# Loading weight chunks in pairs, converting their bits in 1024 columns, and giving block 0 six first steps of FFN1

## The chip, the cores and the metric
The kernel runs on one core of a Trainium2 chip. The metric is the device time in microseconds (us); lower is better. Every time here comes from the chip's runs or from the trace of one profiled execution.

## The reference
A masked attention over 4 batches, 8 heads, 576 tokens of 64 dimensions feeds two feed-forward networks, each over 2304 tokens of width 512:

```
scores = q @ k.T / 8 ; heads 0..3: keys 0..31 back ; heads 4..7: every fourth key, 0..127 back
attn   = exp(scores - max) / (sum + 1e-9)
x      = (attn @ v) as [2304, 512]
h = x @ w_in                                   # FFN1, 512 -> 2048
g = where(h > 0, h, exp(min(h, 0)) - 1)
x = g @ w_out                                  # 2048 -> 512
out = ((x @ w_a) * (x @ w_b)) @ w_out2         # FFN2, 512 -> 1536 -> 512
```

q, k and v are float32; the weights reach the kernel as float64.

## The kernel before, in words
**Tiles and stages.** The tokens are cut into 6 blocks of 384. Attention works per block and head pair p (4 pairs, two heads each), FFN1 per block and column chunk f of 128 (16 chunks). One step (block, f) of FFN1 is 12 matmuls of 384 columns into one PSUM tile (`h1_mm`, L656), the ELU on ScalarE and VectorE (relu L678, exp L679, maximum L684, then a split of g into a high and a low part, L667 and L669), and two steps later 12 matmuls into the block's four output tiles (`y1_mm`, L703). Three products (high·high, high·low, low·high) make up each matmul of the reference, which is why a step has 24. FFN2 (L1123, L1458) follows on all blocks with fewer products by a Strassen-like scheme.

**Order of FFN1.** `STEPS1` lists the steps: block 0 does its first SPLIT steps, then block 1 all 16, then block 0 the rest, then blocks 2 to 5. The weights of chunk f, ("1i", f) of w_in and ("1o", f) of w_out, are loaded and converted for the first SPLIT chunks during block 0's steps, for the others during block 1's.

**Converting weights.** A raw chunk of 128x512 float64 numbers (512 KB) comes as two words each into a tile `wraw`, four of which exist. `bits` makes float32 of it in five instructions of 512 columns: magnitude of the high word (ScalarE, L281), low word scaled (ScalarE, L286), clamp (VectorE, L291), join of both words (VectorE, L296), sign (VectorE, L299). Then the high part (ScalarE, L307) and the low part (VectorE, L321 or L1003) go into a tile `w`. Up to SPLIT the chunks are converted at steps written in the code (`w_convert`), later ones by a planner that fills each step's room on ScalarE and VectorE (`Op`, `COST`, `ROOM`, `tick`), keeping the planned load ahead of use. FFN2's weights go through the same planner and then into combinations that the scheme needs.

**Attention.** Blocks 0 and 1 are the "early" ones, 2 to 5 "steady". For each pair there are scores (early L429, steady L603), softmax, transposes (L515, L623), a copy pt of them (ScalarE, L521), values (L539, L639), and a split of the result into x's high part (ScalarE, L556) and low part (VectorE, L557). In early scores and values, as in steady scores, a matmul reads one half of the 128 partitions, and the program's text alternates between halves. In early values the two halves write two tiles (`banks`). At which FFN1 step each piece is put in is set by the tables B1, B2, B3 and by `end` for the transposes of block 1, which come at end + 1, and its values, at end + 2. For pairs 2 and 3 of block 1, b0 is 1 and 2.

**Order on the engines.** Within and between these places a scheduler arranges the instructions of the program, so that neighbouring groups may be cut and interleaved; the final order on an engine is not that of the text. PE runs its queue in that order.

Of the kernel before, what the change touches and what calls it, by code (L numbers as in the profile page):

```python
# [26 lines left out]
TB = 384  # L27
# [9 lines left out]
SPLIT = 7  # L37
# [9 lines left out]
NRAW = 4  # L47
# [7 lines left out]

C1, C0, AHEAD, LAG_IN, LAG_OUT = SPLIT, NF1 + SPLIT, 56, 3, 1
# [185 lines left out]
def banded_attention_two_ffn(ctx: ExitStack, tc: tile.TileContext, ins, out):  # L242
# [20 lines left out]

    def w_load(key, behind=None):
        kind, f = key
        raw = pm.tile([128, 512, 2], U32, tag="wraw", name="wraw", bufs=NRAW)
        if behind is not None:
            with tc.issue_after(behind):
                G.memset(raw[:, :1, 0], 0)
        SP.dma_start(  # L270
            out=raw.rearrange("p f h -> p (f h)"), in_=ins["w" + kind][f].bitcast(U32)
        )
        w_raw[key] = raw
# [37 lines left out]
    def w_convert_parts(key, pool, on):  # L311

        raw = w_raw.pop(key)
        t = pm.tile([128, 512], U32, tag="wt", name="wt", bufs=4)
        w = pools[pool].tile([128, 2, 512], F32R, tag="w", name="w")
        w_sb[key] = w
        steps = bits(raw[:, :, 1], raw[:, :, 0], t, on[0])
        t = t.bitcast(F32)
# [4 lines left out]
        return [*steps, lambda: part_hi(on[1], w[:, 0, :], t), lower]  # L323

    def w_convert(keys, pool, on):

        for steps in zip(*[w_convert_parts(key, pool, on) for key in keys]):
            for step in steps:
                step()
# [22 lines left out]
    early = Env("at0", ps0, n_early, "right")  # L352
    m_at = [0, 128 + TB, 128 + 2 * TB, ins["masks_e"].shape[1]]
# [418 lines left out]
    free = ["w"] * 11  # L772
# [19 lines left out]
    y2_t = {}  # L792

    def y2_temp(S, op):
        if S and op == "t4":
            y2_t[op] = [pm.tile([128, 512], F32, tag="wt", name="yt", bufs=4) for _ in range(2)]
        elif S:
            y2_t[op] = pm.tile([128, 2, TB], F32, tag="wraw", name="yt", bufs=NRAW)
# [101 lines left out]
    n_free, tail = {"wraw": NRAW, "wt": 4}, [False]  # L900
# [91 lines left out]
    def chunk_ops(key):  # L992

        at = {}
        x = assembly(at)(key)

        def hi():
            at["to"] = pools["wb"].tile([128, 2, 512], F32R, tag="w", name="w")
            part_hi("A", at["to"][:, 0, :], at["t", key])

        def lo():
            w = w_sb[key] = at["to"]
            V.tensor_tensor(w[:, 1, :], at["t", key], f32(w[:, 0, :]), op=SUB)  # L1003

        give("wraw", x)
        give("wt", Op("V", 512, lo, Op("A", 512, hi, x)))

    def assembly(at):
        def assemble(key):
# [3 lines left out]
            def load():  # L1013
                raw = pm.tile([128, 512, 2], U32, tag="wraw", name="wraw", bufs=NRAW)
                SP.dma_start(
                    out=raw.rearrange("p f h -> p (f h)"),
                    in_=ins["w" + key[0]][key[1]].bitcast(U32),
                )
                at["raw", key] = raw

            def high():
                raw = at["raw", key]
                t = pm.tile([128, 512], U32, tag="wt", name="wt", bufs=4)
                chunk.extend(bits(raw[:, :, 1], raw[:, :, 0], t, "A"))
                at["t", key] = t.bitcast(F32)
                at["w", key] = raw.rearrange("p f h -> p (f h)").bitcast(F32)
# [11 lines left out]
    def unit_ops(j):  # L1038
# [17 lines left out]
        def combine(M):  # L1056
# [14 lines left out]
            def spare2():  # L1071
                if "hi" not in at:
                    at["hi"] = pm.tile([128, 512], U32, tag="wt", name="wt", bufs=4).bitcast(F32)
                return at["hi"]

            def spare3():
                if "hi3" not in at:
                    at["hi3"] = pm.tile([128, 512], U32, tag="wt", name="wt", bufs=4).bitcast(F32)
                return at["hi3"]

            on = ON3[M]
            at.pop("hi", None)
            x0, x1 = assemble(k0), assemble(k1)
            if M == "o":
                s1 = add(0, lambda: t(0, 1), lambda: t(0, 0), SUB, x0, x1)
# [4 lines left out]
            else:  # L1090
                s1 = add(0, lambda: t(1, 0), lambda: t(1, 1), ADD, x0, x1)
# [190 lines left out]
    o_ps, o_acc = {}, {}  # L1282
# [64 lines left out]
    def o_parts(S, j, first, last):  # L1347
# [35 lines left out]
        def temp(name):  # L1383
            t = o_acc[name] = pm.tile([128, 512], F32, tag="wt", name="ot", bufs=4)
            return t
# [454 lines left out]
```

## Time and profile before

| | us |
|---|---|
| median of 3 runs | 888.05 (887.69 to 888.75) |
| profiled execution | 887.98 |
| its span | 886.1 |
| PE busy | 879.5 (99%) |
| VectorE busy | 645.2 (73%) |
| ScalarE busy | 499.6 (56%) |

The 1.9 us by which the execution exceeds its span lie around the work that the trace records. PE is TensorE's matmuls, DVE is VectorE, ACT is ScalarE, POOL is GpSimd. A timeline's row is a run of instructions of one kind: its start, its duration to the end of the last one, and in brackets idle time and who ended it. The last matmul's end overlaps the next row's start, so that the price of a group on PE is best read from start to start. The attention's float32 matmuls of scores and values appear as two passes each in the trace, so that a group of 12 has a count of 24; in the order they are counted once.

### The profile page before, as it was taken

Reading aid. Unit: us, or ns where it says so; the run is one execution under the profiler, and the core shown is the slowest. Engines: PE = TensorE matmul, PEld = TensorE weight load, DVE = VectorE, ACT = ScalarE, POOL = GpSimd, SP = SyncE. Lnnn points to the kernel's source line nnn. Section 1 sums busy time; section 2 is a strip of 40 time slices with the busy share of each in tenths; the row PEclk is TensorE's granted clock in tenths of the full one; section 3 lists DMA queues with packets and bytes.
Section 4 is the critical chain, followed back from the end, with each engine's and each line's share of the span. In section 5 each row is a group of like instructions: output and inputs, shape, how many; then the busy total and the mean of one; then the engine's idle time right before and its main releaser. Section 6 shows DMA issues by size and latency. Waiting matters only on the chain.

```text
span 886.1 us, 17826 instructions
## 1 busy us (share of the span) xinstructions
PE 879.5 (99%) x6669; PEld 850.8 (96%) x6669; DVE 645.2 (73%) x1160; ACT 499.6 (56%) x1214; POOL 223.4 (25%) x219
## 2 busy tenths in 40 slices
PE   8999999999999999999999999999999999999998
PEld 5799999999999999999999999999999999999998
DVE  6998997786777777776885556698656698656666
ACT  6897897866767776677764332236332225332231
POOL 1000012332222332322322222222522222522223
PEclk9999999999999999999999999999999999999999
DMA  8865654766556665548997777767777664777712
GB/s 317 296 204 182 185 182 156 226 217 229 185 185 207 209 196 196 188 132 280 327 352 277 235 252 249 247 217 245 256 279 251 248 204 166 264 267 251 249 68 72
DMA packets 76247, 198.21 MB, mean 224 GB/s; under 512 B 8320, under 2 KB 22656, under 8 KB 76160
## 3 DMA queue, kind: packets, MB, share of 16 engines
q1 hardware_dynamic: 66944, 182.64, 60.9%
q10 hardware_dynamic: 9216, 14.42, 4.8%
q8 instruction: 53, 0.87, 0.4%
q14 instruction: 34, 0.28, 0.1%
HBM read 153.51 MB, written 43.52 MB: 222 GB/s over the span
## 4 chain that ended last, share of the span: by engine, by line
PE 96%; ACT 1%; DVE 1%; DMA 1%; issue 0%; SPq 0%; POOL 0%; DVEq 0%; POOLq 0%; ACTq 0%
PE ps_h L1123 30%; PE ps_h L656 22%; PE ps_y L703 22%; PE ps_o L1458 14%; PE ps_v L639 2%; PE ps_s L603 1%; PE ps_t L623 1%; PE ps_o L1318 1%; PE ps_v L539 1%; DMA qk<-in_qk_d 1%; PE ps_s L429 0%; PE ps_v L502 0%; PE ps_t L515 0%; ACT w L307 0%; ACT e L463 0%
## 5 line engine op out<-in xcount | busy, mean ns | idle before, releaser
L1123 PE MATMUL ps_h<-y,w 128*128 128x384 f32 x1512 | 291.4, 336 | 0.0
L1123 PEld LDWEIGHTS ps_h<-y,w 128*128 128x128 f32 x1512 | 256.5, 188 | 1.4 <-DVE el L1178 0.6
L656 PE MATMUL ps_h<-x,w 128*128 128x384 f32 x1152 | 221.6, 339 | 0.5 <-ACT x L556 0.4
L703 PE MATMUL ps_y<-g,w 128*128 128x384 f32 x1152 | 221.3, 339 | 0.0
L656 PEld LDWEIGHTS ps_h<-x,w 128*128 128x128 f32 x1152 | 199.2, 188 | 3.2 <-ACT x L556 0.7
L703 PEld LDWEIGHTS ps_y<-g,w 128*128 128x128 f32 x1152 | 199.7, 188 | 2.5 <-ACT el L678 0.9
L1458 PE MATMUL ps_o<-w,g 128*128 128x256 f32 x1071 | 152.3, 281 | 0.0
L1458 PEld LDWEIGHTS ps_o<-w,g 128*128 128x128 f32 x1071 | 146.6, 188 | 0.2 <-POOL g L1165 0.2
L669 POOL TENSOR_TENSOR g<-el,g 128x384 fp32r<-128x384 f32 x73 | 80.0, 1096 | 208.1 <-ACT g L667 179.0
L684 DVE SCALAR_TENSOR_TENSOR el<-el,ps_h 128x384 f32<-128x384 f32 x96 | 52.9, 551 | 74.1 <-ACT el L679 73.7
L678 ACT ACTIVATE el<-ps_h 128x384 f32<-128x384 f32 x96 | 46.7, 487 | 49.3 <-PE ps_h L656 49.2
L1481 DVE TENSOR_TENSOR acc<-acc,ps_o 128x512 f32<-128x512 f32 (+1 forms) x77 | 49.6, 644 | 33.9 <-PE ps_o L1458 33.7
L1165 POOL TENSOR_TENSOR g<-el,g 128x384 fp32r<-128x384 f32 x34 | 38.9, 1145 | 124.5 <-ACT g L1164 93.3
L406 POOL TENSOR_TENSOR e<-e,rs 128x288 f32<-128x288 f32 (+1 forms) x32 | 25.9, 809 | 151.1 <-DVE rs L405 151.1
L667 ACT ACTIVATE g<-el 128x384 fp32r<-128x384 f32 x96 | 49.6, 516 | 23.9 <-DVE el L684 23.6
L299 DVE SCALAR_TENSOR_TENSOR wt<-wraw,wt 128x512 uint32<-128x512 uint32 x68 | 57.9, 856 | 0.7
L679 ACT ACTIVATE el<-el 128x384 f32<-128x384 f32 x96 | 50.5, 526 | 2.3
L296 DVE SCALAR_TENSOR_TENSOR wt<-wt,wraw 128x512 uint32<-128x512 uint32 x68 | 46.4, 688 | 3.9 <-ACT wraw L286 0.7
L1174 ACT COPY el<-ps_h 128x384 f32<-128x384 f32 x36 | 17.3, 480 | 54.0 <-PE ps_h L1123 51.8
L397 ACT ACTIVATE e<-e,nm 128x96 f32<-128x96 f32 (+1 forms) x96 | 36.3, 380 | 18.9 <-DVE nm L395 18.8
L281 ACT ACTIVATE wt<-wraw 128x512 f32<-128x512 f32 x68 | 45.3, 666 | 2.4 <-DMA wraw<-in_w1i 2.3
L1213 DVE TENSOR_TENSOR u<-ps_h,u 128x384 f32<-128x384 f32 x36 | 20.0, 557 | 34.1 <-PE ps_h L1123 34.0
(120 smaller groups left out, 1034.0 us busy)
## 6 DMA issues: line engine op xcount, KB each, us to landing
w<-w2P_o SPq DMA_DIRECT2D x52, 512.0 KB, 5.8
w<-w2P_a SPq DMA_DIRECT2D x48, 512.0 KB, 4.3
w<-w2P_b SPq DMA_DIRECT2D x48, 512.0 KB, 4.5
wraw<-in_w1i SPq DMA_DIRECT2D x16, 512.0 KB, 3.6
wraw<-in_w1o SPq DMA_DIRECT2D x16, 512.0 KB, 3.6
wraw<-in_w2a SPq DMA_DIRECT2D x12, 512.0 KB, 4.2
wraw<-in_w2b SPq DMA_DIRECT2D x12, 512.0 KB, 4.3
wraw<-in_w2o SPq DMA_DIRECT2D x12, 512.0 KB, 4.5
```

The source lines that it names most:

```text
L296: V.scalar_tensor_tensor(t, t, 3, L, op0=ALU.logical_shift_left, op1=ALU.bitwise_or)
L299: V.scalar_tensor_tensor(t, H, 0x80000000, t, op0=ALU.bitwise_and, op1=ALU.bitwise_or)
L656: T.matmul(ps[:, :TB], w[:, wi, kc * 128 : (kc + 1) * 128], xs[kc][:, xi, :], start=(n == 0), stop=(n == 3 * KC - 1),)
L667: A.activation(g[:, 0, :], gf, AF.Copy)
L669: last_lo[0] = eng.tensor_tensor(g[:, 1, :], gf, f32(g[:, 0, :]), op=ALU.subtract)
L678: A.activation(e, ps[:, :TB], AF.Relu, scale=-1.0)
L679: last_e[0] = A.activation(e, e, AF.Exp, scale=-1.0)
L684: last_g[0] = V.scalar_tensor_tensor(e, e, -1.0, h_ps.pop(s)[:, :TB], op0=ALU.add, op1=ALU.max)
L703: T.matmul(y_ps[t][c][:, :TB], w[:, wi, c * 128 : (c + 1) * 128], g[:, gi, :], start=(first and n == 0), stop=(last and n == 2),)
L1123: last_mm[0] = T.matmul(ps[:, :TB], w[:, wi, kc * 128 : (kc + 1) * 128], y2[S, yop][kc][:, xi, :], start=(start and n == 0), stop=(n == 5) ...
L1458: T.matmul(ps[:, 256 * n : 256 * n + 256], g[name][:, gi, i * 128 : (i + 1) * 128], w[:, wi, h, :], start=((first or not held) and n == m ...
L1481: V.tensor_tensor(a, a, ps[:, :n], op=ADD)
```

## The change
Raw chunks are loaded two into one tile: two tiles of [128, 2, 512, 2] in place of four of [128, 512, 2], with a second pool of two such tiles while block 0's first steps run. `mates` says which two chunks share a tile. The five bit instructions run once for both chunks, over 1024 columns; the split into high and low parts stays at 512 columns per chunk. The planner takes two chunks at a time, with costs for 1024 columns. SPLIT falls from 7 to 6, and with it the number of early `w` tiles from 16 to 14. The temporaries of FFN2 take halves of the new tiles. Block 1's `end` for its pairs 2 and 3 falls by one step. The core of the diff:

```diff
-SPLIT = 7
+SPLIT = 6
...
-NRAW = 4
+NPAIR = 2
...
+    def mates(key):
+
+        kind, f = key
+        if key in (("1i", SPLIT), ("1i", SPLIT + 1)):
+            return ("1i", SPLIT), ("1i", SPLIT + 1)
+        if kind == "i" or kind == "1i" and f < 2:
+            return ("1i", 0), ("1i", 1)
+        if key in (("1o", SPLIT - 2), ("1o", SPLIT - 1)):
+            return ("1o", SPLIT - 2), ("1o", SPLIT - 1)
+        f -= 2 * (kind == "1i")
+        return ("1o", f), ("1i", f + 2)
...
+        ks = mates(key)
+        if ks not in w_raw:
+            here, there = (pm, {"bufs": NPAIR}), (pools["raws"], {})
+            pool, n = there if ks[0] in EXTRA else here
+            w_raw[ks] = pool.tile([128, 2, 512, 2], U32, tag="wraw", name="wraw", **n)
+        raw = w_raw[ks][:, ks.index(key)]
...
+    def pair_convert_parts(ks, pool, on):
+
+        raw, t = w_tiles(ks)
+        steps = bits(raw[..., 1], raw[..., 0], t, on[0])
+        split = zip(*[split_parts(k, t[:, i].bitcast(F32), pool, on) for i, k in enumerate(ks)])
+        return [*steps, *[fn for fns in split for fn in fns]]
...
+        if keys[0] in ONE or mates(keys[0]) != tuple(keys):
+            parts = zip(*[w_convert_parts(key, pool, on) for key in keys])
+            steps = [step for steps in parts for step in steps]
+        else:
+            steps = pair_convert_parts(tuple(keys), pool, on)
+        for step in steps:
+            step()
...
+    pools["raws"] = ps0.enter_context(tc.tile_pool(name="raws", bufs=NPAIR, side="right"))
...
-    free = ["w"] * 11
+    free = ["w"] * 9 + ["wb"] * 2
...
-    COST = {("A", 512): 0.67, ("V", 512): 0.7, ("G", 512): 1.45}
+    COST = {("A", 1024): 1.1, ("V", 1024): 1.22}
...
-        give("wt", Op("V", 512, lo, Op("A", 512, hi, x)))
+        give("wt", *[split(key) for key in keys])
...
+                raw = pm.tile([128, 2, 512, 2], U32, tag="wraw", name="wraw", bufs=NPAIR)
+                for i, key in enumerate(keys):
+                    SP.dma_start(
+                        out=raw[:, i].rearrange("p f h -> p (f h)"),
+                        in_=ins["w" + key[0]][key[1]].bitcast(U32),
+                    )
+                at["raw", keys] = raw
...
-            b = Op("A", 512, high, a, takes="wt")
-            c = Op("A", 512, lambda: chunk[1](), b)
+            b = Op("A", 1024, high, a, takes="wt")
+            c = Op("A", 1024, lambda: chunk[1](), b)
             d = Op("V", 512, lambda: chunk[2](), b)
-            e = Op("V", 512, lambda: chunk[3](), c, d)
-            return Op("V", 512, lambda: chunk[4](), e)
+            e = Op("V", 1024, lambda: chunk[3](), c, d)
+            return Op("V", 1024, lambda: chunk[4](), e)
 
...
+    later_keys = []
     for f in range(NF1):
         st = f
         ks = [("1o", f)]
         if f + 2 < (SPLIT if f < SPLIT else NF1):
             ks.append(("1i", f + 2))
         if f >= SPLIT:
-            for k in ks[::-1]:
-                chunk_ops(k)
+            later_keys.extend(ks)
+            if len(later_keys) > 1:
+                chunk_ops(tuple(later_keys[::-1]))
+                later_keys.clear()
...
             if t < EARLY:
-                end = b0 + 1 + int(b0 >= 0)
+                end = b0 + 1
```

The scheduler's order on PE, first block 1's values of pairs 2 and 3 (ps_v names the tiles, one for each half of the partitions; pt the transposed weights of attention; ps_y and ps_h FFN1's sums). Before, the transposes and the values of pair 2:

```order
L515 MATMUL ps_t_1038<-ident_82,e_822 128x128 x3
L539 MATMUL ps_v_1044<-pt_993,v_879 64x32 x12
L539 MATMUL ps_v_1045<-pt_993,v_879 64x32 x12
L703 MATMUL ps_y_859<-g_954,w_958 128x384 x2
L703 MATMUL ps_y_860<-g_954,w_958 128x384 x2
```

A little later, those of pair 3:

```order
L703 MATMUL ps_y_862<-g_954,w_958 128x384 x3
L539 MATMUL ps_v_1120<-pt_1042,v_935 64x32 x2
L539 MATMUL ps_v_1121<-pt_1042,v_935 64x32 x2
L539 MATMUL ps_v_1120<-pt_1042,v_935 64x32 x2
L539 MATMUL ps_v_1121<-pt_1042,v_935 64x32 x2
```

After:

```order
L554 MATMUL ps_t_961<-ident_82,e_813 128x128 x3
L578 MATMUL ps_v_967<-pt_915,v_863 64x32 x12
L742 MATMUL ps_y_846<-g_882,w_886 128x384 x3
L578 MATMUL ps_v_968<-pt_915,v_863 64x32 x12
L742 MATMUL ps_y_847<-g_882,w_886 128x384 x3
L578 MATMUL ps_v_1041<-pt_965,v_917 64x32 x12
L695 MATMUL ps_h_1077<-x_653,w_117 128x384 x2
L578 MATMUL ps_v_1042<-pt_965,v_917 64x32 x12
L695 MATMUL ps_h_1077<-x_653,w_117 128x384
```

The group of pair 2 (1044, 1045) is now two groups of 12 with FFN matmuls between, and the group of pair 3, which alternated between 1120 and 1121, is two groups of 12 of one tile each (1041, 1042).

PE again, at the scores of block 3's second pair (64x96). Before:

```order
L703 MATMUL ps_y<-g,w 128x384 x12
L656 MATMUL ps_h<-x,w 128x384 x12
L603 MATMUL ps_s<-qk 64x96 x12
L703 MATMUL ps_y<-g,w 128x384 x12
L656 MATMUL ps_h<-x,w 128x384 x12
```

After:

```order
L742 MATMUL ps_y<-g,w 128x384 x12
L695 MATMUL ps_h<-x,w 128x384 x9
L642 MATMUL ps_s<-qk 64x96 x6
L742 MATMUL ps_y<-g,w 128x384 x2
L695 MATMUL ps_h<-x,w 128x384
L742 MATMUL ps_y<-g,w 128x384 x4
L695 MATMUL ps_h<-x,w 128x384 x2
L642 MATMUL ps_s<-qk 64x96 x6
L742 MATMUL ps_y<-g,w 128x384 x6
```

The 12 matmuls of the scores are now 6 and 6, one head in each, with nine FFN matmuls between; the third pair's (64x128) are cut in the same way.

VectorE, in the last steps of block 1's FFN1, from a step's maximum on (el) to the low parts of w. Before:

```order
L684 SCALAR_TENSOR_TENSOR el<-el,ps_h 128x384
L291 TENSOR_SCALAR wt<-wt 128x512 x2
L296 SCALAR_TENSOR_TENSOR wt<-wt,wraw 128x512
L299 SCALAR_TENSOR_TENSOR wt<-wraw,wt 128x512
L405 RECIPROCAL rs<-rs 128x3
L669 TENSOR_TENSOR g<-el,g 128x384
L684 SCALAR_TENSOR_TENSOR el<-el,ps_h 128x384
L1003 TENSOR_TENSOR w<-wt,w 128x512
```

After:

```order
L723 SCALAR_TENSOR_TENSOR el<-el,ps_h 128x384
L308 TENSOR_SCALAR wt<-wt 128x1024
L434 TENSOR_REDUCE nm<-e 128x3
L313 SCALAR_TENSOR_TENSOR wt<-wt,wraw 128x1024
L708 TENSOR_TENSOR g<-el,g 128x384
L1048 TENSOR_TENSOR w<-wt,w 128x512
L444 RECIPROCAL rs<-rs 128x3
L316 SCALAR_TENSOR_TENSOR wt<-wraw,wt 128x1024
L1048 TENSOR_TENSOR w<-wt,w 128x512
```

The clamp, join and sign of two chunks are now one instruction each, and a row reduction of the attention stands between the clamp and the join.

## Rows read from the trace of the kernel before

**Rows 1.** Windows, 112:136: length, busy us (count) PE PEld DVE ACT POOL, clock, DMA share, GB/s.
```profile
112.00:136.00 24.00, 24.00 (x179) 23.51 (x172) 22.92 (x49) 23.55 (x65) 3.05 (x4) 1.00 0.51 165
```

**Rows 2.** Waits of PE: what waits, on what; us in total, times, longest.
```profile
PE ps_h L656 <- ACT x L556: 0.4, 1, 0.4
```

**Rows 3.** PE timeline, 32 to 68 us: start, duration, engine, line, operation, shape, count [idle].
```profile
32.42 0.77 PE L656 MATMUL ps_h<-x,w 128*128 128x384 f32 x3
33.31 0.52 PE L515 MATMUL ps_t<-ident,e 128*128 128x128 f32 x3
...
49.41 1.90 PE L703 MATMUL ps_y<-g,w 128*128 128x384 f32 x10
51.14 0.49 PE L515 MATMUL ps_t<-ident,e 128*128 128x128 f32 x3
...
65.14 1.90 PE L703 MATMUL ps_y<-g,w 128*128 128x384 f32 x10
67.16 0.61 PE L656 MATMUL ps_h<-x,w 128*128 128x384 f32 x2
```

**Rows 4.** PE timeline, the values of block 1's pairs 2 and 3.
```profile
56.19 0.89 PE L539 MATMUL ps_v<-pt,v 64*64 64x32 f32 x24
57.26 0.89 PE L539 MATMUL ps_v<-pt,v 64*64 64x32 f32 x24 [0.18 <-ACT pt L521]
58.08 0.97 PE L703 MATMUL ps_y<-g,w 128*128 128x384 f32 x4
58.89 0.52 PE L656 MATMUL ps_h<-x,w 128*128 128x384 f32 x2
...
61.50 1.03 PE L703 MATMUL ps_y<-g,w 128*128 128x384 f32 x5
62.46 0.90 PE L539 MATMUL ps_v<-pt,v 64*64 64x32 f32 x48
63.30 2.01 PE L656 MATMUL ps_h<-x,w 128*128 128x384 f32 x10
```

**Rows 5.** PE timeline, scores of blocks 2 and 3.
```profile
154.40 1.25 PE L603 MATMUL ps_s<-qk 64*64 64x128 f32 x24
155.59 2.35 PE L703 MATMUL ps_y<-g,w 128*128 128x384 f32 x12
...
165.82 1.03 PE L603 MATMUL ps_s<-qk 64*64 64x96 f32 x24
166.78 2.37 PE L703 MATMUL ps_y<-g,w 128*128 128x384 f32 x12
...
182.26 0.73 PE L603 MATMUL ps_s<-qk 64*64 64x96 f32 x24
182.92 2.37 PE L703 MATMUL ps_y<-g,w 128*128 128x384 f32 x12
...
201.57 0.89 PE L603 MATMUL ps_s<-qk 64*64 64x128 f32 x24
202.39 2.38 PE L703 MATMUL ps_y<-g,w 128*128 128x384 f32 x12
```

**Rows 6.** Timeline of DVE near the end of block 1's FFN1.
```profile
118.00 0.44 DVE L395 TENSOR_REDUCE nm<-e 128x3 f32<-128x288 f32 x1
...
119.68 0.54 DVE L684 SCALAR_TENSOR_TENSOR el<-el,ps_h 128x384 f32<-128x384 f32 x1
120.14 0.75 DVE L291 TENSOR_SCALAR wt<-wt 128x512 f32<-128x512 f32 x2
120.81 0.68 DVE L296 SCALAR_TENSOR_TENSOR wt<-wt,wraw 128x512 uint32<-128x512 uint32 x1
...
122.22 0.53 DVE L669 TENSOR_TENSOR g<-el,g 128x384 fp32r<-128x384 f32 x1
...
123.22 0.69 DVE L1003 TENSOR_TENSOR w<-wt,w 128x512 fp32r<-128x512 f32 x1
```

**Rows 7.** PE timeline, the matmul group at 122.92 us.
```profile
122.92 2.25 PE L656 MATMUL ps_h<-x,w 128*128 128x384 f32 x12
```

More of the change, by code (lines that the diff above doesn't have):

```diff
@@ L270, in w_load @@
         SP.dma_start(
-            out=raw.rearrange("p f h -> p (f h)"), in_=ins["w" + kind][f].bitcast(U32)
+            out=raw.rearrange("p f h -> p (f h)"), in_=ins["w" + key[0]][key[1]].bitcast(U32)
         )
-        w_raw[key] = raw
     ENG = {"A": A, "V": V, "G": G}
@@ L790, in y2_tiles @@
         y2[S, op] = [pool.tile([128, 2, TB], F32R, tag="x", name="y2", **n) for _ in range(2)]
-    y2_t = {}
+    y2_t, y2_half = {}, []
     def y2_temp(S, op):
         if S and op == "t4":
-            y2_t[op] = [pm.tile([128, 512], F32, tag="wt", name="yt", bufs=4) for _ in range(2)]
+            t = pm.tile([128, 2, 512], F32, tag="wt", name="yt", bufs=NPAIR)
+            y2_t[op] = [t[:, i] for i in range(2)]
         elif S:
-            y2_t[op] = pm.tile([128, 2, TB], F32, tag="wraw", name="yt", bufs=NRAW)
+            if not y2_half:
+                t = pm.tile([128, 2, 2, TB], F32, tag="wraw", name="yt", bufs=NPAIR)
+                y2_half.extend([t[:, 1], t[:, 0]])
+            y2_t[op] = y2_half.pop()
         elif op == "t4":
@@ L1005, in chunk_ops, with assemble @@
         give("wraw", x)
-        give("wt", Op("V", 512, lo, Op("A", 512, hi, x)))
+        give("wt", *[split(key) for key in keys])
     def assembly(at):
-        def assemble(key):
+        def assemble(keys):
             chunk = []
             def load():
[L1014 to L1019, printed above, removed]
-            def high():
[L1022 to L1026, printed above, removed]
+                raw = pm.tile([128, 2, 512, 2], U32, tag="wraw", name="wraw", bufs=NPAIR)
[5 more added lines that the diff above has]
+                at["raw", keys] = raw
+            def high():
+                raw = at["raw", keys]
+                t = pm.tile([128, 2, 512], U32, tag="wt", name="wt", bufs=NPAIR)
+                chunk.extend(bits(raw[..., 1], raw[..., 0], t, "A"))
+                for i, key in enumerate(keys):
+                    at["t", key] = t[:, i].bitcast(F32)
+                    at["w", key] = raw[:, i].rearrange("p f h -> p (f h)").bitcast(F32)
@@ L1383, in temp @@
         def temp(name):
-            t = o_acc[name] = pm.tile([128, 512], F32, tag="wt", name="ot", bufs=4)
-            return t
+            if not o_half:
+                t = pm.tile([128, 2, 512], F32, tag="wt", name="ot", bufs=NPAIR)
+                o_half.extend([t[:, 1], t[:, 0]])
+            o_acc[name] = o_half.pop()
+            return o_acc[name]
         def finish(part, ps):
@@ L1596, in first_half @@
     def first_half(keys, on):
-        halves[:] = [w_convert_parts(key, "w", on) for key in keys]
-        for steps in halves:
-            steps.pop(0)()
-            high_done.append(nc.cur_bb.bb.instructions[-1])
+        halves[:] = pair_convert_parts(tuple(keys), "w", on)
+        halves.pop(0)()
+        high_done.append(nc.cur_bb.bb.instructions[-1])
     def second_half():
-        for steps in zip(*halves):
-            for step in steps:
-                step()
+        for step in halves:
+            step()
+    later_keys = []
     for f in range(NF1):
@@ L1631, in pair_begin @@
         with tc.issue_after(x_lo[1, NP - 1].ins):
-            parts = [w_convert_parts(k, "w", ON1) for k in pair]
-            for steps in zip(*[x[:-1] for x in parts]):
-                for step in steps:
-                    step()
-        lowers.extend(x[-1] for x in parts)
+            steps = pair_convert_parts(tuple(pair), "w", ON1)
+            for step in steps[:-2]:
+                step()
+        lowers.extend(steps[-2:])
     def pair_end():
```

79 lines of the change are left out of this document (38 added, 41 removed).

## The prediction

> **What bounds the kernel now.** I read the windows first: busy time of each engine in a stretch. From 112 to 136 us TensorE (PE) is busy for all of 24.00 us, at the granted clock 1.00, while VectorE has 22.92 and ScalarE 23.55 us of work [rows 1]. So PE sets the end, and the other two have a tenth of a microsecond to spare in a few places of the first 140 us. What the change does to them counts only where PE then waits. The list of waits confirms it: the longest that ends on data after the start-up is 0.4 us, on an x that ScalarE copies [rows 2]. The PE timeline then gives two things: the price of each kind of group, read as start of the next row less start of this one (a row's own duration also holds the pipeline's tail), and where a group takes longer than another of its kind.
>
> One matmul of 384 columns costs (51.14−49.41)/10 = 0.173 us [rows 3]; this is the unit below.
>
> **Waits that go.** Three places behind 30 us take longer than their matmuls do.
> (a) Three matmuls from 32.42 to 33.31: 0.89 us [rows 3], against 3×0.173 = 0.52 and 0.10 for the switch priced below. Wait 0.27.
> (b) The values of block 1's head pair 2 (24 matmuls, which the trace records as two passes each): the first 24 passes, 56.19 to 57.26: 1.07 us; the next 24, 57.26 to 58.08: 0.82 [rows 4]. Wait 0.25; its row names ScalarE's copy of pt, which came only then.
> (c) Ten matmuls from 65.14 to 67.16: 2.02 us [rows 3], against 1.73: 0.29, which is block 1's x of its last pair.
> In the new order block 0 hands over one step (24 matmuls, 24×0.173 = 4.15 us) earlier, and the transposes and values of pairs 2 and 3 stand one step earlier too. That takes each wait's producer out of the last place: the order puts FFN matmuls between the producers and their users where before they followed at once. I take all three as gone: 0.27+0.25+0.29 = −0.81. Bounds: 0 (all come back elsewhere, because ScalarE and VectorE do the same work) and −0.81. What is late next at (c) is VectorE's low part of that x; in the new order it has the two halves of FFN work ahead as cover, a few tenths.
>
> **Values of block 1, pairs 2 and 3.** The order before has pair 2 as 12+12 matmuls in a row and pair 3 as one group that alternates between two tiles; the new order has four groups of 12, each of one tile, with FFN matmuls between. One tile's group takes its keys from one half of the partitions. The prices are in the trace: 24 passes of one half took 0.82 us, and pair 3's 48 passes that alternate halves 62.46 to 63.30 = 0.84 [rows 4]. So half the work costs as much as the whole once halves are kept apart. A switch between FFN and these small matmuls costs 61.50 to 62.46 less 5×0.173, 0.10 us on entry, and 58.08 to 58.89 less 4×0.173, 0.12 on leaving [rows 4]: 0.21 for a cut (0.96−0.865+0.81−0.692).
> Pair 3: 2×0.82+0.21−0.84 = +1.01. Pair 2: its halves were apart already, so only the cut, +0.21. Together +1.22. One switch less elsewhere (scores of pair 3 are now followed by transposes at once): −0.10.
>
> **Scores of block 3.** Pairs 1 and 2 are cut too, 12 into 6+6, each six of one head, so of one half of the partitions. No row shows such a half. Whole groups take 182.26 to 182.92 = 0.66 (96 columns) and 201.57 to 202.39 = 0.82 (128 columns) [rows 5]. Bounds: a half costs half, and a cut only its 0.21, so +0.42 for both; or a half costs what the whole did, as the values' rows say: (0.66+0.21)+(0.82+0.21) = +1.90. I take the second, since the values are the nearest rows: same 64 partitions, same alternation, and there the half took 0.82 of 0.84.
>
> The Trainium skill, "TensorE: Matmul & The Clock Gate", Part 3, what overlaps and what doesn't, says that a weight load overlaps a running matmul only when the row group differs. By that rule six matmuls of one head lose the overlap and the sum stays at +1.90; without it the term would be +0.42. The trace agrees on the values (0.82 against 0.84 us); for scores no row here shows it.
>
> **Scores that waited.** Two earlier groups hold waits inside: 154.40 to 155.59 = 1.19 against 0.82 of the same shape, and 165.82 to 166.78 = 0.96 against 0.66 [rows 5], 0.37 and 0.30. The new order has the first 14 and the second 6 FFN matmuls later (2.4 and 1.0 us), more than each waited: −0.67. Bounds: −0.67 and 0.
>
> **Conversions.** Two chunks now share the instructions for 1024 columns. In the order VectorE has 95 instructions fewer and ScalarE 58; each pair saved is about one fixed part of an instruction, which is time of engines that are not the bound [rows 1]: 0 at the end. Its price would lie in delay: a wide instruction can't be passed. The loads are the same DMAs into half as many, twice as large tiles; at a DMA share of 0.51 [rows 1] I cost them at 0, covered by the lead with which chunks are loaded. In block 1's last steps this cover is thin. The low part of the last input chunk stands behind the ELU's maximum of step 19, which begins at 119.68 and ends at 120.22, and in the new order a clamp, a row reduction, a join and a product lie between [rows 6]. With each wide one as two narrow by duration: 0.75+0.44+2×0.68+0.53 = 3.08, plus 0.69 for itself: 123.99. Between starts the rows are shorter than by duration, 0.46 against 0.54 for the maximum (119.68 to 120.14) and 0.67 against 0.75 for the clamps (to 120.81), 0.08 each; five of them make it 123.59, and the two wide ones save a fixed part each on top. The chunk is needed at the third matmul of the group at 122.92: 122.92+2×0.173 = 123.27 [rows 7]. So the bounds are 0 (it is in time) and +0.72; I take 0, which is nearer to the rows by starts less what the wide ones save. FFN2's units and temporaries come from halves of tiles; PE has no wait there and their operations are fewer: 0.
>
> **Sum.** −0.81+1.22−0.10+1.90−0.67+0 = +1.54. The profiled execution took 887.98 us, 0.07 under the median of 888.05; 887.98+1.54 = 889.52, so 889.5, that is 0.16% above before. 0.2% (1.78 us) is about what a measurement of this kernel can tell from no change, so the verdict would most likely be the same. The likeliest case's own range is 888.9 to 890.3: one of the waits stays, or one score cut is cheaper.
>
> **Rivals.**
> 1. Score halves cost half. For it: PE's score groups write both heads to separate tiles anyway, and no row shows a half. Against it: the values. Then +0.42 in place of +1.90: +0.06, 888.0.
> 2. Conversions come late in block 1, the side on which it is slower. The place is the last input chunk's low part; it decides from the point where the maximum of step 19 ends later than about 120.2 us or the wide clamp and join together take over 2 us: from there each microsecond of delay is one at the end. For it: VectorE and ScalarE have 22.92 and 23.55 of 24 us [rows 1], and the buffers come free by pairs. Against it: fewer instructions. The upper bound gives +0.72, 890.2; where the second pair's sign comes ahead as well (one more wide one, 2×0.7) 891.6; I put the case at 890.9. The Trainium skill, "Perfetto Trace Analysis", Optimizing Scalar/DVE Operations, advises both ways: grouping where the engine is saturated, breaking up where an engine that isn't makes others wait. With VectorE at 22.92 of 24 us the trace fits the first, which is why this rival gets little.
> 3. The change doesn't do what the earlier hand-over promises: the five waits come back at other places. Then +1.54+0.81+0.67 = +3.02, 891.0.
> 4. The cuts are free, because the new order has filled gaps that would have been waits otherwise: −0.81−0.10−0.67 = −1.58, 886.4.
>
> **How the numbers follow.** Forecast 0.50 (a third of it over 889.83, where 0.2% begins: slower 0.16, same 0.34). Rival 1: 0.22 (faster 0.02, same 0.20). Rival 2: 0.12 (slower 0.11, same 0.01). Rival 3: 0.09 (slower). Rival 4: 0.07 (faster 0.04, same 0.03). So faster 0.06, same 0.58, slower 0.36. The range: rivals 1 and 2 belong in it, the tails of 3 and 4 not: 887.9 to 891.4.
>
> **What would show it.** In the profile after: the values of pairs 2 and 3 of block 1 as four groups of 24 passes, each of about 0.82 us; block 3's two cut score pairs as groups of 12 passes of 0.66 and 0.82 us (rival 1: 0.33 and 0.41); x waits and the pt wait missing from the list of waits; the two earlier score groups at 0.82 and 0.66. Rival 2 is a PE wait on a low part or on an ELU near 120 us. The prediction is wrong if PE waits anew for more than a microsecond anywhere behind 60 us, or if time in FFN2 moves at all.

## The result and the profile after

The changed kernel takes 892.92 us (median of 6 runs, 891.71 to 895.77) beside 888.02 for the kernel before (6 runs); the ratio is 1.0056, with a 95% interval of 1.0045 to 1.0067. That is 4.9 us more, where 1.5 was forecast, and above the range. The profiled execution took 893.18 us, with a span of 891.4.

The page after, engines first (busy us, share, instructions):

```profile
PE 883.0 (99%) x6669; PEld 853.0 (96%) x6669; DVE 618.1 (69%) x1065; ACT 493.8 (55%) x1153; POOL 235.2 (26%) x220
```

VectorE and ScalarE are busy for 27 and 6 us less than before, as the wide instructions promise, and none of that reaches the end. The window that answers to [rows 1]:

```profile
112.00:136.00 24.00, 22.92 (x170) 21.86 (x169) 22.98 (x38) 21.37 (x50) 2.91 (x3) 1.00 0.45 168
```

PE has lost 1.08 us there, and VectorE is as full as before with 11 instructions fewer. The waits of PE, to be held against [rows 2]:

```profile
PE ps_v L578 <- issue: 1.7, 1, 1.7
...
PE ps_h L695 <- DVE w L1048: 1.1, 1, 1.1
PE ps_h L695 <- ACT x L595: 0.4, 1, 0.4
PE ps_h L1159 <- ACT el L1210: 0.2, 1, 0.2
```

The list is short and the time is 5 us, so a second measure is needed. Both kernels issue the same number of FFN matmuls (4959, counted over L695, L742, L1159, L1354 and L1498), so the n-th of them can be compared with the n-th of the first profile of before. The growth of that lag over a stretch is what the stretch lost. The borders lie at 32.00, 67.44, 125.75, 171.24, 211.00, 480.06 and 487.46 us by the clock of before, where the kernels have the same attention work behind them (e3 alone has three transposes more ahead of 125.75):

| us lost in | to 32 | 32 to 67 | 67 to 125 | 125 to 171 | 171 to 211 | 480 to 487 | rest | all |
|---|---|---|---|---|---|---|---|---|
| forecast | 0 | +0.31 | 0 | −0.67 | +1.90 | 0 | 0 | +1.54 |
| changed kernel | 1.01 | 0.12 | 1.35 | 0.21 | 1.81 | 0.49 | 0.30 | 5.30 |
| the same again (e6) | 0.16 | 0.15 | 0.71 | 0.37 | 1.81 | 3.57 | 0.26 | 7.03 |
| before again (e5) | −0.19 | −0.10 | 0 | 0.01 | 0 | 0 | −0.03 | −0.31 |
| e1 late load | −0.07 | 0.14 | 0.86 | 0.25 | 1.81 | 0.17 | 0.17 | 3.32 |
| e2 narrow last pair | 1.86 | 0.14 | 0 | 0.19 | 0.01 | 0.63 | 0.45 | 3.27 |
| e3 hand-over alone | 1.59 | 0.27 | 2.07 | −0.65 | 0 | 0 | 0.22 | 3.49 |
| e4 pairs alone | 0.42 | 0.26 | 1.69 | 0.26 | 0.44 | 0 | −0.07 | 3.00 |
| e7 more room | 0.05 | 0.14 | 3.55 | 0.82 | 1.43 | 0 | 0.26 | 6.26 |
| e8 late load, narrow | −0.13 | 0.14 | 0 | 0.41 | 0.01 | 0.09 | 0.14 | 0.68 |
| e9 copy first | −0.52 | 0.14 | 0.81 | −0.01 | 1.81 | 0 | 0.31 | 2.53 |
| e10 three mends | 0.61 | 0.11 | 0 | 0.29 | 0.01 | 0 | 0.40 | 1.42 |
| e11 hand-over, more room | 0.30 | 0.17 | 0 | −0.37 | 0 | 0 | 0.17 | 0.27 |

The rows below the second are the experiments. Each is one profile, whose run can lie a microsecond or two off the median of its kernel.

**32 to 67 us** came within 0.2 us of the forecast: +0.12 beside +0.31. The values of block 1's pairs 2 and 3, PE's timeline after ([rows 4] before):

```profile
55.74 0.89 PE L578 MATMUL ps_v<-pt,v 64*64 64x32 f32 x24
56.56 0.79 PE L742 MATMUL ps_y<-g,w 128*128 128x384 f32 x3
57.28 0.89 PE L578 MATMUL ps_v<-pt,v 64*64 64x32 f32 x24
58.10 0.79 PE L742 MATMUL ps_y<-g,w 128*128 128x384 f32 x3
58.82 0.89 PE L578 MATMUL ps_v<-pt,v 64*64 64x32 f32 x24
59.63 0.62 PE L695 MATMUL ps_h<-x,w 128*128 128x384 f32 x2
```

These rows show three of the four halves, which take 0.81 to 0.82 us each from start to start (the fourth, at 60.19, takes 0.81 as well). Three FFN matmuls between two of them take 0.72 us, 0.20 more than 3×0.173.

**171 to 211 us** came as forecast, +1.81 beside +1.90. The cut scores of block 3 ([rows 5] before):

```profile
184.44 0.71 PE L642 MATMUL ps_s<-qk 64*64 64x96 f32 x12
185.08 0.62 PE L742 MATMUL ps_y<-g,w 128*128 128x384 f32 x2
...
186.86 0.71 PE L642 MATMUL ps_s<-qk 64*64 64x96 f32 x12
187.50 1.33 PE L742 MATMUL ps_y<-g,w 128*128 128x384 f32 x6
...
205.10 0.87 PE L642 MATMUL ps_s<-qk 64*64 64x128 f32 x12
205.91 0.62 PE L742 MATMUL ps_y<-g,w 128*128 128x384 f32 x2
206.46 0.87 PE L642 MATMUL ps_s<-qk 64*64 64x128 f32 x12
207.26 2.02 PE L742 MATMUL ps_y<-g,w 128*128 128x384 f32 x10
```

Six matmuls of one head take 0.64 us at 96 columns (12 of both: 0.66 before) and 0.80 to 0.81 at 128 (0.82). Half the work costs as much as the whole. The trace's records of single matmuls show why: in the whole group of before four begin within 0.02 us, two passes of each head, and the next four 0.08 us later. In a half only two begin together, and the next two also come 0.08 us later. The halves of the partitions work side by side, and a half alone leaves the other idle.

**67 to 125 us** did not. VectorE's timeline behind the maximum of step 19, which is to be held against [rows 6]:

```profile
119.90 1.69 DVE L316 SCALAR_TENSOR_TENSOR wt<-wraw,wt 128x1024 uint32<-128x1024 uint32 x1
121.51 0.44 DVE L652 SCALAR_TENSOR_TENSOR e<-ps_s,masks 128x288 f32<-128x288 f32 x1
121.88 0.54 DVE L723 SCALAR_TENSOR_TENSOR el<-el,ps_h 128x384 f32<-128x384 f32 x1
...
124.91 0.68 DVE L1048 TENSOR_TENSOR w<-wt,w 128x512 fp32r<-128x512 f32 x1
```

ScalarE meanwhile:

```profile
119.26 0.53 ACT L718 ACTIVATE el<-el 128x384 f32<-128x384 f32 x1
120.57 1.15 ACT L298 ACTIVATE wt<-wraw 128x1024 f32<-128x1024 f32 x1 [0.79 <-DMA wraw<-in_w1o]
121.62 1.13 ACT L303 ACTIVATE wraw<-wraw 128x1024 uint32<-128x1024 uint32 x1
122.64 0.63 ACT L324 ACTIVATE w<-wt 128x512 fp32r<-128x512 f32 x1
```

and PE ([rows 7] before):

```profile
124.05 0.51 PE L695 MATMUL ps_h<-x,w 128*128 128x384 f32 x2
125.64 2.01 PE L695 MATMUL ps_h<-x,w 128*128 128x384 f32 x10 [1.08 <-DVE w L1048]
```

ScalarE ends the exponential at 119.79, but VectorE's next instruction, from 119.90 on, is a sign over 1024 columns, and it comes to the maximum only at 121.88. In before the two instructions ahead of the maximum were narrow:

```profile
118.36 0.79 DVE L299 SCALAR_TENSOR_TENSOR wt<-wraw,wt 128x512 uint32<-128x512 uint32 x1
119.07 0.68 DVE L1003 TENSOR_TENSOR w<-wt,w 128x512 fp32r<-128x512 f32 x1
```

The chunk's high part stands on ScalarE behind two wide instructions of the next pair, the first of which waits 0.79 us for its load. The high part is done at 123.27, VectorE is busy without a gap until it comes to the low part at 124.91, so it is VectorE's queue that decides. The low part ends at 125.59, and PE goes on 0.05 us later.

Some 0.5 us of this wait belongs to the one profile and not to the order. The sign begins 0.28 us after the start of a product on GpSimd, here and in e1, e6 and e9, which have the same order on VectorE. Here the sign took 1.69 us and the product 0.89 (GpSimd's times are rough); in the other three the sign took 1.22 and the product 2.03, and PE waited 0.44 to 0.59 us. First the product of this profile, then product and sign of e1:

```profile
119.62 0.89 POOL L445 TENSOR_TENSOR e<-e,rs 128x288 f32<-128x288 f32 x1 [104.84 <-DVE rs L444]
```

```profile
118.53 2.03 POOL L445 TENSOR_TENSOR e<-e,rs 128x288 f32<-128x288 f32 x1 [103.66 <-DVE rs L444]
118.81 1.22 DVE L316 SCALAR_TENSOR_TENSOR wt<-wraw,wt 128x1024 uint32<-128x1024 uint32 x1
```

One of the two is slowed by the other; what decides which is not shown.

**125 to 171 us.** Of the two waits that were to go, one went (0.82 us for the second group below, in place of 1.19 in [rows 5]), one stayed (1.02 against 0.66 without a wait), and a third group, which took 146.46 to 147.27 before, now takes 1.32:

```profile
148.94 1.39 PE L642 MATMUL ps_s<-qk 64*64 64x128 f32 x24
150.26 2.35 PE L695 MATMUL ps_h<-x,w 128*128 128x384 f32 x12
...
159.79 0.89 PE L642 MATMUL ps_s<-qk 64*64 64x128 f32 x24
160.61 1.32 PE L695 MATMUL ps_h<-x,w 128*128 128x384 f32 x6
...
169.51 1.09 PE L642 MATMUL ps_s<-qk 64*64 64x96 f32 x24
170.53 1.31 PE L742 MATMUL ps_y<-g,w 128*128 128x384 f32 x6
```

**480 to 487 us**, the beginning of FFN2, is where the second profile of the same kernel lost 3.57 us. ScalarE there (e6):

```profile
484.48 0.52 ACT L324 ACTIVATE y<-y 128x384 fp32r<-128x384 f32 x1 [4.21 <-DMA y<-y]
...
485.32 0.51 ACT L324 ACTIVATE y<-y 128x384 fp32r<-128x384 f32 x1
485.74 0.46 ACT L1210 COPY el<-ps_h 128x384 f32<-128x384 f32 x1
```

and PE:

```profile
483.76 0.68 PE L742 MATMUL ps_y<-g,w 128*128 128x384 f32 x3
486.25 3.68 PE L1159 MATMUL ps_h<-y,w 128*128 128x384 f32 x12 [1.80 <-ACT el L1210]
```

The wait is little more than half of what is lost. The 12 matmuls behind it take 3.47 us up to the next row's start, where 12×0.173 are 2.08, since the granted clock of TensorE fell to half (1.2 in place of 2.4 GHz) in that stretch; the window's last numbers are clock, DMA share and GB/s:

```profile
486.20:490.00 3.80, 3.75 (x13) 3.75 (x14) 0.56 (x1) 1.51 (x3) 0.29 (x1) 0.59 0.19 73
```

By the lag some 2.1 of the 3.57 us are the wait and some 1.5 the clock. The clock fell in two more profiles, behind a pause of 1.38 us in e2's start-up (0.61 granted from 20 to 24 us) and behind a wait of 1.85 us in e7; behind a pause of 1.74 in the first profile and of 1.66 in e3 it did not. These three runs have a mean granted clock of 0.998. So have three of the changed kernel's six runs, and a fourth has 0.994, while two of the 59 runs of before with a clock on record and none of e8 to e11 are below 0.999. So part of the 4.9 us is probably this clock; where it fell in the runs without a profile is not recorded.

The copy empties the tile that PE's next group writes. It stands behind a conversion of y that waits for a load. By its tile names this y belongs to FFN2's second half of the tokens, which PE reaches much later. In the order of before the same conversions stand behind the copy:

```
before                                        after
L667 ACTIVATE g<-el 128x384                   L324 ACTIVATE y_6915<-y_6915 128x384
L1174 COPY el<-ps_h 128x384                   L706 ACTIVATE g<-el 128x384
L307 ACTIVATE y_7141<-y_7141 128x384          L324 ACTIVATE y_6916<-y_6916 128x384
L307 ACTIVATE y_7142<-y_7142 128x384          L1210 COPY el<-ps_h 128x384
```

### The profile page after: what moved, and what is told of

Read it like the earlier page. It is cut to its first block, busy times and chain, and to the rows that moved or that the text cites. A ratio compares the mean times of both kernels' runs of the same rounds, so it can differ in the third digit from the quotient of the medians.

```text
span 891.4 us, 17702 instructions
## 1 busy us (share of the span) xinstructions
PE 883.0 (99%) x6669; PEld 853.0 (96%) x6669; DVE 618.1 (69%) x1065; ACT 493.8 (55%) x1153; POOL 235.2 (26%) x220
## 4 chain that ended last, share of the span: by engine, by line
PE 82%; DVE 2%; DMA 2%; ACT 1%; issue 0%; ACTq 0%; POOL 0%; SPq 0%; DVEq 0%
PE ps_h L1159 30%; PE ps_y L742 17%; PE ps_h L695 17%; PE ps_o L1498 14%; PE ps_v L678 1%; PE ps_s L642 1%; DMA wraw<-in_w1o 1%; PE ps_t L662 1%; PE ps_o L1354 1%; DMA y<-y 1%; DVE wt L316 1%; ACT wt L298 0%; DVE wt L313 0%; ACT g L706 0%; DVE el L723 0%
## 5 line engine op out<-in xcount | busy, mean ns | idle before, releaser
L1159 PE MATMUL ps_h<-y,w 128*128 128x384 f32 x1512 | 291.7, 337 | 0.2 <-ACT el L1210 0.2
L1159 PEld LDWEIGHTS ps_h<-y,w 128*128 128x128 f32 x1512 | 256.8, 188 | 1.9 <-DVE el L1214 0.6
L695 PE MATMUL ps_h<-x,w 128*128 128x384 f32 x1152 | 222.5, 340 | 1.5 <-DVE w L1048 1.1
L742 PE MATMUL ps_y<-g,w 128*128 128x384 f32 x1152 | 221.8, 339 | 0.0
L695 PEld LDWEIGHTS ps_h<-x,w 128*128 128x128 f32 x1152 | 199.2, 188 | 4.3 <-DVE w L1048 1.4
L742 PEld LDWEIGHTS ps_y<-g,w 128*128 128x128 f32 x1152 | 199.5, 188 | 2.5 <-ACT el L717 0.9
L1498 PE MATMUL ps_o<-w,g 128*128 128x256 f32 x1071 | 152.4, 281 | 0.0
L1498 PEld LDWEIGHTS ps_o<-w,g 128*128 128x128 f32 x1071 | 146.7, 188 | 0.2 <-POOL g L1201 0.2
L708 POOL TENSOR_TENSOR g<-el,g 128x384 fp32r<-128x384 f32 x74 | 84.7, 1145 | 226.2 <-ACT g L706 182.9
L1201 POOL TENSOR_TENSOR g<-el,g 128x384 fp32r<-128x384 f32 x34 | 38.9, 1144 | 123.3 <-ACT g L1200 93.1
L445 POOL TENSOR_TENSOR e<-e,rs 128x288 f32<-128x288 f32 (+1 forms) x32 | 34.5, 1079 | 127.1 <-DVE rs L444 125.2
L706 ACT ACTIVATE g<-el 128x384 fp32r<-128x384 f32 x96 | 49.9, 520 | 23.8 <-DVE el L723 23.7
L316 DVE SCALAR_TENSOR_TENSOR wt<-wraw,wt 128x1024 uint32<-128x1024 uint32 (+1 forms) x37 | 49.2, 1329 | 0.2
L313 DVE SCALAR_TENSOR_TENSOR wt<-wt,wraw 128x1024 uint32<-128x1024 uint32 (+1 forms) x37 | 42.0, 1137 | 5.7 <-ACT wraw L303 5.0
L1230 ACT COPY u<-ps_h 128x384 f32<-128x384 f32 x36 | 17.2, 479 | 46.7 <-PE ps_h L1159 46.6
L1200 ACT ACTIVATE g<-el 128x384 fp32r<-128x384 f32 x36 | 18.9, 525 | 42.8 <-DVE el L1218 37.0
```

The costliest lines, as they stand in the source:

```text
L313: V.scalar_tensor_tensor(t, t, 3, L, op0=ALU.logical_shift_left, op1=ALU.bitwise_or)
L316: V.scalar_tensor_tensor(t, H, 0x80000000, t, op0=ALU.bitwise_and, op1=ALU.bitwise_or)
L695: T.matmul(ps[:, :TB], w[:, wi, kc * 128 : (kc + 1) * 128], xs[kc][:, xi, :], start=(n == 0), stop=(n == 3 * KC - 1),)
L706: A.activation(g[:, 0, :], gf, AF.Copy)
L708: last_lo[0] = eng.tensor_tensor(g[:, 1, :], gf, f32(g[:, 0, :]), op=ALU.subtract)
L742: T.matmul(y_ps[t][c][:, :TB], w[:, wi, c * 128 : (c + 1) * 128], g[:, gi, :], start=(first and n == 0), stop=(last and n == 2),)
```

## The experiments

The theories as they stood: the additional pair tiles let loads start early and delay the start-up (A); the wide instructions make the last chunk late (B), with the lost step of lead (B1) or the width alone (B2) as its cause; the order on ScalarE costs the time at FFN2's beginning (C).

**e1, the load of chunk 3 held back**

```diff
-                at_step(step, slot, w_load, k)
+                at_step(step, slot, w_load, k, *(signed[:1] if k == ("1i", 3) else ()))
```

> The changed kernel, with the load of w_in's chunk 3 held back until VectorE has done the sign step of the start-up (some 21 us), so that the chunk loads stand on the DMA queues about where they stood before. Theory A (the additional pair tiles let chunk loads start 6 us earlier, the DMA engines are full, and TensorE's own instruction fetch comes a microsecond later): TensorE's pause inside the values at 19 to 20.6 us falls from 1.74 to about 0.9 us, and the time by 0.8 to 1.1, to 891.8 to 892.1. Rival (the fetch moves by a microsecond from run to run, whatever is loaded): the pause stays where it was and the time at 892.9.

891.22 us, ratio 1.0034 (1.0023 to 1.0046); the pause was 0.9 us. The time fell by more than theory A had said. It looked like theory A; e3, e5 and e6 took it back.

**e2, the last input chunk's pair narrow**

```diff
+NARROW = lambda keys: ('1i', 15) in keys
...
-        x = assembly(at)(keys)
+        x = assembly(at)(keys) if NARROW is None or not NARROW(keys) else narrow(at, keys)
```

`narrow` loads the two chunks into one tile and issues the five steps over 512 columns for each.

> The changed kernel, but the pair that holds the last chunk of w_in is converted in instructions of 512 columns; it is still loaded into one tile. In the order the scores of block 3 are then not cut any more either. Theory B (the wide sign of the pair before and the wide clamp and join stand in front of a maximum and of the last low part): the wait of 1.1 us at 124 us goes, and with the uncut scores 1.8 us: 892.9-1.2-1.8 = 889.9. Rival (half as many raw tiles, so that the chunks arrive late whatever the width): the wait at 124 us stays above 0.5 us, 891 or more.

889.49 us, 1.0010 (1.0001 to 1.0020). PE waits nowhere from 67 to 125 us and the scores are whole: both terms are 0 in the table. VectorE's end of the chunk:

```profile
117.19 0.68 DVE L317 SCALAR_TENSOR_TENSOR wt<-wraw,wt 128x512 uint32<-128x512 uint32 x1
...
121.87 0.80 DVE L1049 TENSOR_TENSOR w<-wt,w 128x512 fp32r<-128x512 f32 x1
```

The chunk's sign ends at 117.87, where the wide one ended at 121.59, and its low part at 122.67, where PE's group begins at 124.91. Theory B holds for this chunk; the rival, half as many raw tiles, falls for it, since the tiles are the same. The edit changes the width of five steps and, through the planner and the scheduler, also the places of others on VectorE and of the scores on PE; the two effects are not separated.

**e3, the hand-over alone**

```diff
-SPLIT = 7
+SPLIT = 6
...
-    free = ["w"] * 11
+    free = ["w"] * 9 + ["wb"] * 2
...
-                end = b0 + 1 + int(b0 >= 0)
+                end = b0 + 1
```

> The kernel before, with block 0 handing over after six steps, block 1's transposes and values one step earlier and two w tiles fewer in the early pool, but single chunks and 512 columns. Theory (the earlier hand-over is nearly neutral: three waits of 0.81 us go, one cut of values of 0.2 us comes): 887.2 to 888.2, no wait near 124 us. Rival (one step of lead less for the last chunk is enough to make it late, whatever the width): a wait of 0.5 us or more near 124 us, 889 or more.

890.47 us, 1.0021 (1.0010 to 1.0031): the rival in its time. Without any wide instruction PE waits for a low part, one step ahead of the one that the rival named, and then for an attention whose softmax is late:

```profile
121.74 2.02 PE L656 MATMUL ps_h<-x,w 128*128 128x384 f32 x10 [0.61 <-DVE w L1003]
...
125.06 0.51 PE L623 MATMUL ps_t<-ident,e 128*96 128x128 f32 x3 [0.65 <-DVE e L613]
```

Of the 2.07 us lost 0.65 comes back behind it, at the two score groups of [rows 5] that waited in before: PE comes 3.9 and 3.6 us later to them, and they take 0.82 and 0.65 us. That is the gain of 0.67 which the prediction had expected from moving them, and here they have not moved. Its start-up, with the loads as before, has the pause of 1.7 us: theory A is in doubt.

**e4, the pairs alone** (the changed kernel with SPLIT 7, 16 early w tiles and the old `end`)

> The changed kernel with seven steps of block 0, sixteen early w tiles and block 1's transposes and values at the old step: pair loading and wide conversion alone. Theories A and B: the start-up is about 1 us longer as in the changed kernel, the last chunk has one more step of lead and there is no wait of over 0.3 us near 124 to 130 us, scores and values are not cut: 888.8 to 889.4. Rival to A: the start-up as before, 888.0 to 888.4. Rival to B (pairs alone make the chunk late): a wait of 0.5 us or more there, 889.5 or more.

890.91 us, 1.0031 (1.0021 to 1.0042). No wait near 124 us, but 1.69 us go in block 1 all the same, 0.9 us of it at 84 us, at this wait, and the rest in small pieces of 0.1 to 0.3 us at other steps:

```profile
PE ps_y L742 <- DVE g L708: 0.6, 1, 0.6
```

So each part alone makes VectorE late for PE in block 1, at another place each time. The rival to B was right in its time and wrong in its place.

**e5 and e6, both kernels once more**

> The kernel before, unchanged, for one more profile. It tells how far the start-up moves by itself. Theory A (the fetch of TensorE's instructions is late because of the changed kernel's additional early chunk loads): the pause inside the values at about 19 us is 0.9 to 1.0 us as in the first profile. Rival (it moves from run to run, as the 1.7 us of the hand-over alone suggest, which loads as before): it differs from the first by 0.3 us or more.

> The changed kernel, unchanged, for one more profile. Theory A: the pause at 19 us is 1.6 to 1.8 us again. Rival: it differs from the first by 0.3 us or more. What belongs to the order stays in either case: 1.3 us lost between 67 and 125 us, 1.8 us at the two cut scores, 0.2 around the scores before, 0.5 to 0.8 from the beginning of FFN2 on.

887.57 and 894.99 us, one run each. The pause was 0.7 us in before, and in the changed kernel (first profile, then this one):

```profile
20.57 0.77 PE L578 MATMUL ps_v<-pt,v 64*64 64x32 f32 x35 [1.74 <-issue]
```

```profile
19.69 0.77 PE L578 MATMUL ps_v<-pt,v 64*64 64x32 f32 x35 [0.93 <-issue]
```

The same program pauses 1.74 and 0.93 us: the rival, and theory A falls. In the trace's DMA records a fetch of 16 KB on the instruction queue lands 1.3 to 1.5 us ahead of the end of this pause in all 13 profiles (18.05 and 19.51 in before, 19.16 and 20.57 after, 19.61 and 21.13 in e3). It moves by up to 1.9 us, with no relation to which kernel loads what: to 32 us, kernels with late loading lost −0.07, −0.13 and 0.61, single chunks −0.19, 1.59 and 0.30, early pairs between −0.52 and 1.86 (the last, e2, with the clock at half). What sets its time stays open.

Of what was expected to stay, the cut scores did (1.81). Block 1 lost 0.71 in place of 1.3, the scores before 0.37 in place of 0.2, and the loss from 480 us on was 3.57 in place of at most 0.8.

**e7, more room for the planner**

```diff
-ROOM1 = {"V": 1.75, "A": 1.3, "G": 0.9}
+ROOM1 = {"V": 1.95, "A": 1.45, "G": 0.9}
```

> The changed kernel with more room for the planner in block 1's steps (1.95 and 1.45 us a step for VectorE and ScalarE in place of 1.75 and 1.3), which by the order puts the last input chunk's low part a step earlier; the instructions stay 1024 wide, and two score pairs are cut as before, the first of them earlier. Theory B1 (the lost step of lead makes the chunk late): the wait at 124 us goes, 892.9-1.3 = 891.6. Theory B2 (the width alone does it, whatever the lead): a wait of 0.8 us or more on a low part stays, 892.5 or more.

893.74 us, 1.0062 (1.0045 to 1.0079): no gain, so with wide instructions B1 falls; B2 is right in its time, but PE now waits for the high part, by ScalarE:

```profile
125.13 3.27 PE L695 MATMUL ps_h<-x,w 128*128 128x384 f32 x12 [1.85 <-ACT w L324]
```

The clock fell here too (0.65 granted from 125 to 129 us), which makes about 1.5 of the 3.55 us in the table; the three runs without a profile had the clock whole and took 893.20 to 894.46, so the verdict does not rest on it. With wide instructions an earlier plan did not help. Ahead of that high part ScalarE did a softmax's exponentials and an ELU, and the wide sign that it needs ended at 123.25; which of the two made it late is not separated.

**e8, late load and narrow pair**

> The narrow last pair and the late load of chunk 3 together. Theory A (each removes its own loss): 889.5 less 0.5 to 1.1 of the start-up, 888.4 to 889.0, the same as before within 0.1%. Rival (the late load gains nothing on average): 889.3 to 889.7.

889.17 us, 1.0014 (1.0005 to 1.0024), between the two forecasts and not distinguishable from e2: a gain of the late load is not shown.

**e9, the copy first**

```diff
-        for kc in range(2):
-            part_hi(hi[kc], y2[S, op][kc][:, 0, :], src[kc])
+        with tc.issue_after(copy0[0].ins) if S and copy0 else nullcontext():
+            for kc in range(2):
+                part_hi(hi[kc], y2[S, op][kc][:, 0, :], src[kc])
...
-                A.copy(p, z[:, :TB])
+                copy0.append(A.copy(p, z[:, :TB]))
```

> The changed kernel with one ordering: at the beginning of FFN2 the two conversions of y for FFN2's second half, which wait for their loads, come behind the first copy of a sum, on which TensorE waits for a free tile, as in the kernel before. Theory C (the loss there, 0.5 to 0.8 us in one profile and 3.8 in the other, is this order on ScalarE): the loss from 480 us on falls to 0.3 us or less and the time by 0.5 to 2, to 891 to 892.4 or, as a ratio to the kernel before, 1.0030 to 1.0050. Rival (TensorE then waits for the load itself or for another instruction): 1.0 us or more is lost there as before.

890.73 us, 1.0031 (1.0019 to 1.0042). The loss from 480 to 487 us is 0.00 in the table, in e10 and e11 too. That alone would not prove it, since e4 and e7 have the conversions ahead of the copy and lose nothing either: there the loads had landed early enough for PE. ScalarE after the edit:

```profile
481.40 0.48 ACT L1213 COPY el<-ps_h 128x384 f32<-128x384 f32 x1 [0.83 <-PE ps_h L1162]
481.77 1.97 ACT L324 ACTIVATE y<-y 128x384 fp32r<-128x384 f32 x4
```

The copy's row waits for PE and no longer stands behind a load. Theory C holds: the order on ScalarE decides whether PE depends on a load.

**e10, three mends** (e8 with the copy first)

> The changed kernel with the narrow last pair, the late load of chunk 3 and the copy first. If the three losses add up, what is left is the cut values (0.4 us), one wait at the scores (0.2 to 0.4) and a few tenths: 888.4 to 889.0 beside 887.9 to 888.4, ratio 1.0005 to 1.0012. If the copy is of no use, as with the late load alone, 1.0014.

888.94 us, 1.0008 (0.9998 to 1.0017), within what was stated, so most of the 4.9 us goes with these edits. How it divides between them the times do not show. By the ratios the narrow pair alone gains 4.1 us against the changed kernel, the copy alone 2.2, and both with the late load 4.3; each is good to little more than a microsecond, and e10 cannot be told from e8. The table shows the losses in block 1, at the cut scores and at FFN2's beginning gone, each at its own place.

**e11, the hand-over with more room, single chunks, copy first**

> The kernel before with the earlier hand-over alone (single chunks, 512 columns), more room for the planner in block 1's steps (1.95 and 1.45 us) and the copy first; by the order the low parts of the last chunks come one to two steps earlier. Theory B1 (the hand-over alone loses 2.8 us in block 1 since a step of lead is gone, and gains 1.4 at the scores behind): the loss in block 1 falls below 0.5 us, the gain at the scores stays, so 0.5 to 1.1 less than before: 887.0 to 887.6, ratio 0.9987 to 0.9994. Rival (the load of the engines, not the lead, sets it, as in the run with more room and pairs): 1.5 us or more is lost in block 1, 888.5 or more.

888.28 us, 1.0004 (0.9995 to 1.0013): the same as before. With narrow instructions more room does what it did not in e7: nothing is lost from 67 to 125 us. But the gain at the scores shrinks from 0.65 to 0.37, and the forecast gain did not come. Its 1.4 was read at a border where e3 had a score group moved across; 0.65 is what the scores gave. With more room and the copy first, the hand-over is neutral. No version here beats the kernel before.

## Why the prediction was wrong

Its terms from the orders of PE came out: cut values and waits of 32 to 67 us +0.31 against 0.12 to 0.15, cut scores +1.90 against 1.81. The rival that a half costs half (0.22) fell. The prediction leaned on the Trainium skill's rule ("TensorE: Matmul & The Clock Gate", Part 3, what overlaps and what doesn't) that a weight load overlaps a running matmul only when the row group differs. The price by that rule came out, 0.64 us for a half against 0.66 for the whole; but by the records it is the matmuls of the two heads that run side by side, and the weight loads of a half still begin while its own matmuls run.

The time lies outside the range because of three terms, of which the first was priced as a rival. The step that failed is the one on conversions, costed at 0; it cost 0.71 to 1.35. It took the ELU's maximum of step 19 from the trace of before, at 119.68 to 120.22, although instructions ahead of it on VectorE had become wide. From the maximum to the low part's end it was right: 122.42 to 125.59 is 3.17 us, against 3.77 by durations and 3.37 less shortened starts. But the maximum began at 121.88, 2.2 us later: 1.1 us of that is the lag up to there, and 1.07 is VectorE, still busy with the wide sign of 1.69 us and a mask step in front of it. In the other three profiles of this order the sign took 1.22, the maximum was late by 0.41 to 0.58 over the lag, and PE waited 0.44 to 0.59. That is rival 2, with its place, its sign and its price (+0.72 to 2.1; 0.71 to 1.35 lost in four profiles of this order), given 0.12 on the argument that there are fewer instructions. Busy time fell and the delay rose. The Trainium skill advises to break up instructions where an engine that is not saturated makes others wait ("Perfetto Trace Analysis", Optimizing Scalar/DVE Operations). The prediction set that aside, because VectorE is busy for 22.92 of 24 us; e2 shows that breaking up helped all the same.

The second failure is a claim that FFN2 costs 0 because PE had no wait there before. A new order of ScalarE's queue made one: seven profiles have the conversions ahead of the copy, and they lost 0.09 to 3.57 us there in five (the changed kernel twice, e1, e2, e8) and nothing in two (e4, e7). The orders showed it: a copy that PE waits for, behind an instruction that waits for a DMA. The prediction names no order of ScalarE there. It also had no term for TensorE's clock, which made 1.5 of the 3.57.

The third is the gain of 0.67 at the earlier scores, which was a loss of 0 to 0.37 in its place: it counted how far the groups moved against FFN matmuls, but not that what they wait for moved too. The x wait of 0.4 us that it read from [rows 2] is none of its three waits (a) to (c): it stands at 24.26 us, and it stayed.

The sum of typical sizes is 0.14 + 0.93 (mean of four profiles in block 1) + 0.21 + 1.81 + 1.41 (mean of three at FFN2's beginning, e9 left out) + 0.3 in the rest = 4.80, beside 4.9 measured. That it comes so near is partly luck, since the 1.41 is mostly one profile's 3.57. The 0.3 of the rest, 0.1 here and there, was not traced further. Nor is it shown why each part alone loses time in block 1 as well (e3, e4) beyond the waits named.

## What to carry to other kernels

Here fewer, wider instructions on an engine that is 95% busy saved its time and not its user's: an instruction over two units delivers the first only when the second is done, and delays whatever small step the critical engine wants next. When an order is compared, go through the in-order queues of the helpers and look for an instruction that another engine waits for, behind one that waits for a DMA. Where a term is taken from a time of the old trace, ask first what in front of it changed. A forecast wait can cost more than its length: look at the granted clock behind it.

## What was not expected of the hardware

A matmul group that uses one half of the partitions takes as long as a group of both halves with twice the work: 0.64 and 0.66 us at 96 columns, 0.80 and 0.82 at 128, 0.81 and 0.84 at 32. PE's pause at 19 us ends 1.3 to 1.5 us after an instruction fetch of 16 KB lands, and the landing moves by up to 1.9 us between profiles; a kernel's first profile can carry a microsecond that belongs to no edit. Of a sign over 1024 columns on VectorE and a GpSimd product that began 0.28 us before it, once the sign was slow (1.69 us, the product 0.89) and three times the product (2.03, the sign 1.22), with the same order on VectorE each time. A PE wait of 1.80 us was followed by 12 matmuls in 3.47 us at half the granted clock, where they take 2.08.
